# Unit 2's hidden sums in an output bank pair, all of w_out scaled by GpSimd and loaded later, and another order of the first chunk's taps, in the start of a fused convolution and feed-forward kernel

## The chip, the cores and the metric

One core of one Trainium2 chip. The metric is the device time of one execution in microseconds (us), as the median of several runs; lower is better. All runs compared here are fast (granted TensorE clock 0.999 to 1.0).

## The reference

```python
# x: (8, 4096, 192); weight: (8 heads, 7 taps); w_in: (192, 2048); w_out: (2048, 192); beta: (2048,)
w = softmax(weight, axis=-1)                    # 7 taps per head
c = causal convolution of x with w along the sequence, each head's 24 channels with its own taps
h = c.reshape(32768, 192) @ w_in
g = h / (1 + exp(-beta * h))
out = g @ w_out
```

## The kernel before

The 32768 tokens are done in 32 chunks of 1024 (512 tokens of each of two halves of the batch). For a chunk the kernel makes `ct`, the convolution, as three groups of channels. Then come 16 units: a unit is six matmuls of `ct` with 128 columns of `w_in` (*hidden*), one Silu on ScalarE over 128 x 1024 values, and *pairs* of output matmuls with `w_out`. `Silu(beta*h)` is beta times what is wanted, so `w_out` is divided by beta once, at the start (*scaling*, in four pieces).

From chunk 2 on VectorE alone makes the convolution, 7 *taps* per chunk, and a transposing DMA delivers its input. Chunks 0 and 1 are made otherwise: x is transposed on TensorE, and taps are matmuls with a diagonal matrix (chunk 0: groups 1 and 2 and part of group 3; chunk 1: group 1, called *conv1* below).

PSUM is handed out as four pairs of banks: two `ph` for the hidden sums, and `pa` and `pb` for output sums. At the start `pa` and `pb` also serve as places for transposes and taps. In the traces each engine's instructions start in the order of the Python code (in the changed kernel TensorE starts conv1's taps at 17.11 us and unit 5, which stands behind them in the code, at 18.36), so that order is what the change moves.

The parts that the change touches (cut, marked by `...`):

```python
    # loads, in this order
    ...
    for i in range(NW - 1):
        load_w_out(i)
    load(2)                      # x of the third chunk
    load_w_out(NW - 1)
    load(3)
    ...
    new_ct(0)
    for c in range(NG - 1):                                # groups 1 and 2: 7 taps on TensorE each
        pv = in_b() if c else psum_h.tile([128, 2, TOK], FP32, name="ph")
        for k in range(K):
            diag_tap(k, xt0[:, c], pv[:, 0, :])
        ...
        nc.scalar.copy(cts[0][:, c, :], pv[:, 0, :])
    ...
    K_V = 5                                                # group 3: 5 taps on VectorE, 2 on TensorE
    pv = in_a()[:, 0, :]
    for k in range(K_V, K):
        diag_tap(k, xt0[:, NG - 1], pv, k0=K_V)
    ...
    nc.vector.tensor_tensor(dst, pv, dst, ALU.add)
    ...
    scale_w_out(0)                                         # GpSimd
    scale_w_out(1)                                         # GpSimd
    ...
    CONV1 = {4: (1, 3), 5: (3, 5), 6: (5, K)}              # conv1's taps, after which unit
    ...
    first_work = {                                         # chunk 0, VectorE's work, after which unit
        4: [None, None],                                   # None: a tap of chunk 1
        5: [None],
        6: [conv1_evac, lambda: scale_w_out(2), None],     # scale 2 and 3: VectorE
        7: [None, lambda: rows_of(2)],                     # cast and transpose the third chunk
        8: [lambda: scale_w_out(3), None],
        9: [None],
    }
    QUOTA_A = {4: 2, 7: 4, 8: 4}                           # output pairs in units 4, 7, 8
    ...
            if s == 0 and u == min(CONV1):
                conv1(0, 1)                                # conv1's first tap, in front of unit 4
```

Of the kernel before, what the change touches and what calls it, by code (L numbers as in the profile page):

```python
# [9 lines left out]
FP32 = mybir.dt.float32  # L10
# [7 lines left out]
def kernel(  # L18
# [62 lines left out]
    def in_a():  # L81
        return psum_a.tile([128, 2, TOK], FP32, name="pa")

    def in_b():
        return psum_b.tile([128, 2, TOK], FP32, name="pb")
# [5 lines left out]
    def load(ch):  # L91
        p, c = divmod(ch, CHUNKS)
        xf = xf_pool.tile([128, 2, NB, D], FP32, name="xf")
        for h in range(2):
            nc.sync.dma_start(
                out=xf[:, h],
                in_=x_v[p, c * TOK : (c + 1) * TOK, h, :].rearrange(
                    "(b q) d -> q b d", q=BLK
                ),
            )  # L100
        xfs[ch] = xf
# [9 lines left out]
    def new_xt(ch):  # L111
        xt = xt_pool.tile([128, NG, HALO + TOK], BF16, name="xt")
        xts[ch] = xt
        return xt
# [31 lines left out]
    def load_w_out(i):  # L146
        fcs = slice(i * NQ, (i + 1) * NQ)
        nc.sync.dma_start(out=w_out_raw[:, fcs, :], in_=w_out_v[:, fcs, :])
# [19 lines left out]
    for r in range(2):  # L168
        nc.sync.dma_start(out=w_in_raw[r * DG : (r + 1) * DG], in_=w_in_v[:, :, 0:F0])
    load_x(x1, TOK, 1)  # L170
    for i in range(NW - 1):
        load_w_out(i)
    load(2)
    load_w_out(NW - 1)
    load(3)

    zeros = setup.tile([128, 128], BF16)
    nc.vector.memset(zeros, 0.0)
# [46 lines left out]
    def cast_rows(copy, xb, x, b):  # L225
        copy(  # L226
            xb[:, b].rearrange("q c h p -> q h c p"),
            x[:, b // 2, :, b % 2].rearrange("q h (p c) -> q h c p", c=NG),
        )
# [46 lines left out]
    for i in range(1, NW):  # L276
        load_w_in(i * FW, (i + 1) * FW)

    xt1 = setup.tile([128, HALO + TOK], FP32R)
    cts = {}  # L280

    def new_ct(s):
        cts[s] = ct_pool.tile([128, NG, TOK], BF16, name="ct")

    def diag_tap(k, xt, pv, rows=slice(0, 128), k0=0):
        o = HALO - PAD + k
        nc.tensor.matmul(  # L287
            pv,
            diag[rows, k, :],
            xt[rows, o : o + TOK],  # L290
            start=(k == k0),
            stop=(k == K - 1),
        )
# [17 lines left out]

    def scale_w_out(i):
        fcs = slice(i * NQ, (i + 1) * NQ)
        (nc.vector if i > 1 else nc.gpsimd).tensor_tensor(  # L314
            w_out_s[:, fcs, :],
            w_out_raw[:, fcs, :],
            beta_r[:, fcs].unsqueeze(2).to_broadcast((128, NQ, D)),
            ALU.mult,
        )


    new_ct(0)
    for c in range(NG - 1):
        pv = in_b() if c else psum_h.tile([128, 2, TOK], FP32, name="ph")
        for k in range(K):
            diag_tap(k, xt0[:, c], pv[:, 0, :])
        if c == 0:
            for b in range(2):
                cast_rows(nc.scalar.copy, x1b, x1, b)
        nc.scalar.copy(cts[0][:, c, :], pv[:, 0, :])  # L330
        if c == 0:
            nc.scalar.copy(w_in_s[:, :, 0:F0], w_in_raw)
    cast_rows(nc.scalar.copy, x1b, x1, 2)

    def tap(dst, src, k):
        scalar = cw[:, k : k + 1]
        if k == 0:
            nc.vector.tensor_scalar_mul(dst, src, scalar)  # L338
        else:
            nc.vector.scalar_tensor_tensor(  # L340
                out=dst, in0=src, scalar=scalar, in1=dst, op0=ALU.mult, op1=ALU.add
            )

    K_V = 5
    pv = in_a()[:, 0, :]
    for k in range(K_V, K):
        diag_tap(k, xt0[:, NG - 1], pv, k0=K_V)
    dst = cts[0][:, NG - 1, :]
    for k in range(K_V):
        o = HALO - PAD + k  # L350
        tap(dst, xt0[:, NG - 1, o : o + TOK].bitcast(FP32), k)
    nc.vector.tensor_tensor(dst, pv, dst, ALU.add)
    cast_rows(nc.vector.tensor_copy, x1b, x1, 3)
    nc.vector.reciprocal(beta_r, beta)  # L354
    scale_w_out(0)
    scale_w_out(1)


    def second():
        xt = new_xt(1)  # L360
        for i in range(2):
            pt = (in_b, in_a)[i]()
            for b in range(2):
                for c in range(NG):
                    for r in range(2):
                        rows = slice(r * DG, (r + 1) * DG)
                        o = (c * 2 + b) * DG
                        nc.tensor.matmul(
                            pt[:, r, o : o + DG],
                            x1b[rows, 2 * i + b, c].rearrange("q h p -> q (h p)"),  # L370
                            ident_b[rows, rows],
                            start=True,
                            stop=True,
                        )
            t = HALO + i * 2 * BLK
            for r in range(2):
                nc.vector.tensor_copy(
                    xt[:, :, t + r * BLK : t + (r + 1) * BLK].rearrange(
                        "p c (q b) -> p c q b", b=2
                    ),  # L380
                    pt[:, r, 0 : NG * BLK].rearrange("p (c b q) -> p c q b", c=NG, b=2),
                )
        halo(1, xt0)
        nc.vector.tensor_copy(xt1[:, HALO - PAD :], xt[:, 0, HALO - PAD :])


    CONV1 = {4: (1, 3), 5: (3, 5), 6: (5, K)}
    conv1_ps = []

    def conv1(k0, k1):  # L390
        if not conv1_ps:
            new_ct(1)
            conv1_ps.append(in_b())
        pv = conv1_ps[0]
        for k in range(k0, k1):
            for r in range(2):
                diag_tap(k, xt1, pv[:, r, :], slice(r * DG, (r + 1) * DG))
# [15 lines left out]

    gs = {}

    def hidden(s, fc, js=range(NG), ph=None):
        if fc == 0 and s not in gs:
            gs[s] = g_pool.tile([128, NF, 2, TOK], BF16, name="g")
        if ph is None:
            ph = psum_h.tile([128, 2, TOK], FP32, name="ph")  # L420
        for j in js:
            for h in range(2):
                rows = slice(h * DG, (h + 1) * DG)
                nc.tensor.matmul(  # L424
                    ph[:, h, :],
                    w_in_s[rows, j, fc * 128 : (fc + 1) * 128],
                    cts[s][rows, j, :],
                    start=(j == 0),
                    stop=(j == NG - 1),
                )  # L430
            if j == NG - 1:
                nc.scalar.activation(  # L432
                    gs[s][:, fc], ph, AF.Silu, scale=beta[:, fc : fc + 1]
                )
        return ph
# [86 lines left out]
    def rows_of(ch):  # L522
        for h in range(2):
            cast(ch, h)
        xpose(ch)
# [1 line left out]

    first_work = {
        4: [None, None],
        5: [None],  # L530
        6: [conv1_evac, lambda: scale_w_out(2), None],
        7: [None, lambda: rows_of(2)],
        8: [lambda: scale_w_out(3), None],
        9: [None],
    }

    QUOTA_A = {4: 2, 7: 4, 8: 4}
    queue = deque()
    for s in range(N_ST):
        jobs_of(s)  # L540
        for u in range(NF):
            if s == 0 and u == min(CONV1):
                conv1(0, 1)
            if s > 0 or u > 1:
                hidden(s, u)
            elif u == 0:
                phs = [hidden(0, fc, [0]) for fc in range(2)]
                for j in range(1, NG):
                    for fc in range(2):
                        hidden(0, fc, [j], phs[fc])  # L550
                second()
            if s > 0:
                output(s, u, 8 if s < N_ST - 1 else 6, "ab")
            elif u > 8:
                output(s, u, 5 if u < NF - 1 else 10, "ab")
            elif u in QUOTA_A:
                output(s, u, QUOTA_A[u], "a")
            if s == 0:
                if u in CONV1:
                    conv1(*CONV1[u])  # L560
                if u == min(CONV1):
                    queue.extend(conv_ops(1, 1))
                for work in first_work.get(u, []):
                    (work or queue.popleft())()
            else:
                if u % 2 and queue:
                    queue.popleft()()

                if u == 0 and s + 3 < N_CH:
                    load(s + 3)  # L570
                if u < 2 and s + 2 < N_CH:
                    cast(s + 2, u)
                if u == 1 and s + 2 < N_CH:
                    xpose(s + 2)
            if u == 12 and s + 2 < N_CH:
                queue.extend(conv_ops(s + 2, 0))
# [32 lines left out]
```

## Time and profile before

| | before |
|---|---|
| median time | 690.51 us (3 runs, 690.11 to 690.86); 690.43 (4 runs) with one more later |
| span of the profiled run | 688.0 us |
| TensorE busy | 99% |
| first tap on TensorE | 7.21 us |
| first Silu of chunk 0 / 1 / 2 | 12.65 / 30.25 / 51.23 us |
| every later chunk | 20.92 us per chunk |

The page's top and the head of the chain that ended last:

```profile
span 688.0 us, 24344 instructions
...
PE 682.2 (99%) x11312; PEld 521.1 (76%) x11312; DVE 524.7 (76%) x467; ACT 579.0 (84%) x530; POOL 9.9 (1%) x20
...
PE 98%; DMA 1%; ACT 0%; DVE 0%; issue 0%; ACTq 0%
```

TensorE (PE) ends last at nearly every step. A unit in the steady state is 0.65 us of hidden matmuls and 0.66 us of output matmuls. The change can only win what TensorE loses before it reaches that state, in the first 30 us. TensorE there, from the timeline (start, duration, engine, line, operation, tiles, count; in brackets the idle time before it and what ended it):

```profile
13.82 0.82 PE L424 MATMUL ph<-ct,w_in_s 64*128 64x512 bf16 x6 [0.70 <-ACT g L432]
14.82 0.82 PE L424 MATMUL ph<-ct,w_in_s 64*128 64x512 bf16 x6 [0.18 <-ACT g L432]
...
15.62 0.49 PE L287 MATMUL pb<-xt,diag 64*128 64x512 f32 x2
```

Units 2 and 3 wait 0.70 and 0.18 us for Silu to free a `ph` pair. The last line is conv1's first tap, which stands in front of unit 4. ScalarE (ACT) in the same stretch:

```profile
12.65 5.28 ACT L432 ACTIVATE g<-ph,beta 128x1024 bf16<-128x1024 f32 x5 [0.70 <-PE ph L424]
18.14 11.76 ACT L432 ACTIVATE g<-ph,beta 128x1024 bf16<-128x1024 f32 x11 [0.20 <-PE ph L424]
30.25 1.11 ACT L432 ACTIVATE g<-ph,beta 128x1024 bf16<-128x1024 f32 x1 [0.36 <-PE ph L424]
```

The first five Silus run without idle time. VectorE (DVE), GpSimd (POOL) and the DMA issues of the third chunk's transposes (SPq):

```profile
11.42 0.69 DVE L352 TENSOR_TENSOR ct<-pa,ct 128x512 bf16<-128x512 f32 x1
15.05 0.43 DVE L384 CAST xt<-xt 128x518 fp32r<-128x518 bf16 x1
15.39 1.69 DVE L338 TENSOR_SCALAR ct<-xt,cw 128x1024 bf16<-128x1024 bf16 x1
24.54 1.27 DVE L106 CAST xb<-xf 128x768 bf16<-128x768 f32 x2
32.93 1.00 DVE L338 TENSOR_SCALAR ct<-xt,cw 128x1536 bf16<-128x1536 bf16 x1
```

```profile
15.14 1.66 POOL L314 TENSOR_TENSOR w_out_s<-w_out_raw,beta_r 128x768 bf16<-128x768 f32 x1 [0.99 <-DMA w_out_raw<-in_moe_w_out_dram]
```

```profile
25.84 5.48 SPq L127 DMA_TRANSPOSE xt<-xb x4
```

The third group's sum ends at 12.11 us (11.42 + 0.69); Silu 0 follows at 12.65. The tap at 15.39 took 1.69 us with GpSimd's scaling beside it.

### The profile page before, as it was taken

To read this page: it belongs to the slowest core of one execution; us is meant where nothing else is said; L and a number is where in the kernel's file an instruction comes from. 1 tells how busy PE (TensorE), PEld (TensorE's weight loads), DVE (VectorE), ACT (ScalarE), POOL (GpSimd) and SP (SyncE) were. 2 spreads that over 40 slices of the span, in tenths; PEclk is the share of its full clock that TensorE was granted. 3 is DMA by queue.
4 is the path that set the end of the run, shared out by engine and by line. 5 is a ranking of instruction groups with operands and counts; after the bars stand their busy time and mean duration, and the time that the engine had idled before them with its cause. 6 is when DMAs were issued, how large, how long until landed. Compare 5 with 4: busy or idle time off the path is not lost.

```text
span 688.0 us, 24344 instructions
## 1 busy us (share of the span) xinstructions
PE 682.2 (99%) x11312; PEld 521.1 (76%) x11312; DVE 524.7 (76%) x467; ACT 579.0 (84%) x530; POOL 9.9 (1%) x20
## 2 busy tenths in 40 slices
PE   8999999999999999999999999999999999999998
PEld 4777777777777777777777777777777777777777
DVE  7989877788777787777797777887777977777712
ACT  7988888888888888888888888888888888888893
POOL 5000000000000000000000000000000000000000
PEclk9999999999999999999999999999999999999999
DMA  9734333244332244332444332444323443322111
GB/s 234 190 97 117 105 100 98 58 107 117 101 99 77 77 116 116 95 99 61 98 117 105 93 97 57 116 117 96 103 60 93 117 109 96 100 59 59 49 36 59
DMA packets 121861, 67.06 MB, mean 97 GB/s; under 512 B 53264, under 2 KB 121760, under 8 KB 121760
## 3 DMA queue, kind: packets, MB, share of 16 engines
q1 hardware_dynamic: 120048, 64.12, 34.7%
q0 software_dynamic: 1664, 1.38, 1.2%
q8 instruction: 88, 1.44, 0.9%
q14 instruction: 13, 0.11, 0.0%
q10 hardware_dynamic: 48, 0.01, 0.0%
HBM read 29.89 MB, written 25.17 MB: 80 GB/s over the span
## 4 chain that ended last, share of the span: by engine, by line
PE 98%; DMA 1%; ACT 0%; DVE 0%; issue 0%; ACTq 0%
PE ph L424 48%; PE pa L457 25%; PE pb L457 24%; DMA x<-in_x_dram 1%; PE pb L287 1%; ACT g L432 0%; PE ph L287 0%; DVE x0b L226 0%; ACT xt L302 0%; PE pa L287 0%; PE pb L233 0%; PE ph L233 0%; DVE diag L260 0%; ACT osb L473 0%; ACT beta L309 0%
## 5 line engine op out<-in xcount | busy, mean ns | idle before, releaser
L432 ACT ACTIVATE g<-ph,beta 128x1024 bf16<-128x1024 f32 x512 | 569.7, 1115 | 94.5 <-PE ph L424 89.8
L457 PEld LDWEIGHTS <-g 64*128 64x128 bf16 x8160 | 370.7, 94 | 102.3 <-issue 0.2
L424 PE MATMUL ph<-ct,w_in_s 64*128 64x512 bf16 x3072 | 424.3, 376 | 0.9 <-ACT g L432 0.9
L340 DVE SCALAR_TENSOR_TENSOR ct<-xt,cw,ct 128x1536 bf16<-128x1536 bf16 (+2 forms) x190 | 336.9, 1773 | 2.5
L457 PE MATMUL pa<-w_out_s,g 64*128 64x192 bf16 x4112 | 244.8, 243 | 0.0
L457 PE MATMUL pb<-w_out_s,g 64*128 64x192 bf16 (+1 forms) x4048 | 230.4, 243 | 0.0
L424 PEld LDWEIGHTS <-w_in_s 64*128 64x128 bf16 x3072 | 159.6, 94 | 54.8 <-issue 2.7
L475 DVE TENSOR_REDUCE osb<-pa 128x384 f32<-128x768 f32 x64 | 61.3, 958 | 122.5 <-PE pa L457 121.1
L475 DVE TENSOR_REDUCE osb<-pb 128x384 f32<-128x768 f32 x63 | 60.3, 957 | 29.1 <-PE pb L457 29.1
L106 DVE CAST xb<-xf 128x768 bf16<-128x768 f32 x60 | 40.5, 677 | 0.0
L338 DVE TENSOR_SCALAR ct<-xt,cw 128x1536 bf16<-128x1536 bf16 (+2 forms) x32 | 32.4, 1011 | 0.0
L473 ACT COPY osb<-pb 128x192 f32<-128x192 f32 x1 | 0.3, 319 | 7.2 <-PE pb L457 7.2
L211 POOL DMA_DIRECT2D w_in_s<-in_moe_w_in_dram x8 | 5.2, 662 | 0.0
L223 PE MATMUL ph<-zeros 128*128 128x512 bf16 (+2 forms) x11 | 4.1, 485 | 1.1 <-DVE warm L180 1.1
L287 PE MATMUL pb<-xt,diag 64*128 64x512 f32 (+1 forms) x21 | 4.7, 443 | 0.0
L121 DVE COPY xt<-xt 128x18 bf16<-128x18 bf16 x27 | 4.4, 164 | 0.0
L287 PEld LDWEIGHTS pb<-xt,diag 64*128 64x128 f32 (+1 forms) x21 | 2.7, 187 | 0.9 <-issue 0.4
L314 POOL TENSOR_TENSOR w_out_s<-w_out_raw,beta_r 128x768 bf16<-128x768 f32 x2 | 3.1, 1564 | 4.1 <-DVE beta_r L354 3.2
L223 PEld LDWEIGHTS <-zeros 128*128 128x128 bf16 x11 | 1.2, 121 | 2.2 <-issue 1.1
L181 ACT ACT_TABLE_LOAD x1 | 1.3, 1283 | 1.8 <-PEq L593 1.8
L226 ACT CAST x1b<-x 128x384 bf16<-128x384 f32 x3 | 2.0, 714 | 0.4 <-DMA x<-in_x_dram 0.4
L287 PE MATMUL ph<-xt,diag 128*128 128x512 f32 x7 | 1.9, 409 | 0.1
(55 smaller groups left out, 26.9 us busy)
## 6 DMA issues: line engine op xcount, KB each, us to landing
out_dram<-osb SPq DMA_DIRECT2D x127, 192.0 KB, 2.2
xf<-in_x_dram SPq DMA_DIRECT2D x60, 384.0 KB, 4.3
xt<-xb SPq DMA_TRANSPOSE x120, 2.6
x<-in_x_dram SPq DMA_DIRECT2D x4, 384.0 KB, 4.9
w_out_raw<-in_moe_w_out_dram SPq DMA_DIRECT2D x4, 384.0 KB, 13.5
w_in_s<-in_moe_w_in_dram POOLq DMA_DIRECT2D x6, 192.0 KB, 10.5
w_in_raw<-in_moe_w_in_dram SPq DMA_DIRECT2D x2, 192.0 KB, 5.6
w_in_s<-in_moe_w_in_dram POOLq DMA_DIRECT2D x2, 96.0 KB, 7.4
```

The source lines that it names most:

```text
L106: nc.vector.tensor_copy(xbs[ch][:, :, :, h, :], xfs[ch][:, h].rearrange("q b (p c) -> q b c p", c=NG),)
L121: nc.vector.tensor_copy(dst, last[:, :, HALO + TOK - PAD :])
L211: nc.gpsimd.dma_start(out=w_in_s[r * DG : (r + 1) * DG, :, c0:c1], in_=w_in_v[:, :, c0:c1])
L223: nc.tensor.matmul(pf[:, 0, 0:cols], zeros, zc, start=True, stop=True)
L287: nc.tensor.matmul(pv, diag[rows, k, :], xt[rows, o : o + TOK], start=(k == k0), stop=(k == K - 1),)
L314: (nc.vector if i > 1 else nc.gpsimd).tensor_tensor(w_out_s[:, fcs, :], w_out_raw[:, fcs, :], beta_r[:, fcs].unsqueeze(2).to_broadcast((12 ...
L338: nc.vector.tensor_scalar_mul(dst, src, scalar)
L340: nc.vector.scalar_tensor_tensor(out=dst, in0=src, scalar=scalar, in1=dst, op0=ALU.mult, op1=ALU.add)
L424: nc.tensor.matmul(ph[:, h, :], w_in_s[rows, j, fc * 128 : (fc + 1) * 128], cts[s][rows, j, :], start=(j == 0), stop=(j == NG - 1),)
L432: nc.scalar.activation(gs[s][:, fc], ph, AF.Silu, scale=beta[:, fc : fc + 1])
L457: nc.tensor.matmul(self.po[:, r, b * D : (b + 1) * D], g[rows, fc, self.h, q * BLK : (q + 1) * BLK], w_out_s[rows, fc, :], start=(self.don ...
L475: nc.vector.tensor_reduce(dst, self.po[:, :, 0 : nb * D].rearrange("p r n -> p n r"), axis=mybir.AxisListType.X, op=ALU.add,)
```

## The change

Its intent: start unit 0 earlier by taking one of the third group's five taps from VectorE and having TensorE do that group's share before the second group; let unit 0 be finished by itself; give unit 2's hidden sums the free pair `pa`, so that TensorE does not wait for Silu; free VectorE of the last two scalings; and load w_out later, behind what is needed first.

```diff
-    for i in range(NW - 1):
-        load_w_out(i)
-    load(2)
-    load_w_out(NW - 1)
-    load(3)
+    load_w_out(0)
 ...
+    nc.gpsimd.tensor_copy(w_out_raw[:, NQ, 0:1], x1[:, 1, 0, 0, 0:1])   # holds the next loads until x1 is in
+    for i in range(1, NW - 1):
+        load_w_out(i)
+    load(2)
+    load_w_out(NW - 1)
+    load(3)
 ...
-        (nc.vector if i > 1 else nc.gpsimd).tensor_tensor(     # scale_w_out
+        nc.gpsimd.tensor_tensor(
 ...
+    K_V = 4
+    for c, k0 in (0, 0), (2, K_V), (1, 0):                     # group 3's three taps ahead of group 2
+        for k in range(k0, K):
+            diag_tap(k, xt0[:, c], pvs[c], k0=k0)
 ...
+    for i, copy in enumerate((nc.scalar.copy, nc.vector.tensor_copy)):   # group 2's sums, in halves
+        half = slice(i * TOK // 2, (i + 1) * TOK // 2)
+        copy(cts[0][:, 1, half], pvs[1][:, half])
 ...
+    for i in range(NW):
+        scale_w_out(i)
 ...                                      # second chunk's transposes: bf16, all in one pair pb
-    CONV1 = {4: (1, 3), 5: (3, 5), 6: (5, K)}
+    CONV1 = {4: (0, 5), 5: (5, K)}
 ...
-        5: [None],
-        6: [conv1_evac, lambda: scale_w_out(2), None],
-        7: [None, lambda: rows_of(2)],
-        8: [lambda: scale_w_out(3), None],
-        9: [None],
+        5: [None, conv1_evac],
+        6: [None, None],
+        7: [None, None],
+        8: [lambda: rows_of(2)],
-    QUOTA_A = {4: 2, 7: 4, 8: 4}
+    QUOTA_A = {6: 5, 7: 5, 8: 4}
 ...
-            if s == 0 and u == min(CONV1):
-                conv1(0, 1)
 ...
-                phs = [hidden(0, fc, [0]) for fc in range(2)]
-                for j in range(1, NG):
-                    for fc in range(2):
-                        hidden(0, fc, [j], phs[fc])
+                for fc in range(2):
+                    hidden(0, fc, (0, 2, 1))                   # unit 0 by itself, group 2 last
                 second()
+            elif u == 2:
+                hidden(0, u, ph=in_a())
 ...
-                output(s, u, 5 if u < NF - 1 else 10, "ab")
+                output(s, u, 5 if u < NF - 1 else 8, "ab")
```

More of the change, by code (lines that the diff above doesn't have):

```diff
@@ L319, in scale_w_out @@
         )
-    new_ct(0)
-    for c in range(NG - 1):
-        pv = in_b() if c else psum_h.tile([128, 2, TOK], FP32, name="ph")
-        for k in range(K):
-            diag_tap(k, xt0[:, c], pv[:, 0, :])
-        if c == 0:
-            for b in range(2):
-                cast_rows(nc.scalar.copy, x1b, x1, b)
-        nc.scalar.copy(cts[0][:, c, :], pv[:, 0, :])
-        if c == 0:
-            nc.scalar.copy(w_in_s[:, :, 0:F0], w_in_raw)
-    cast_rows(nc.scalar.copy, x1b, x1, 2)
     def tap(dst, src, k):
@@ L342, in tap @@
             )
-    K_V = 5
-    pv = in_a()[:, 0, :]
-    for k in range(K_V, K):
-        diag_tap(k, xt0[:, NG - 1], pv, k0=K_V)
-    dst = cts[0][:, NG - 1, :]
+    new_ct(0)
+    K_V = 4
+    pvs = [
+        psum_h.tile([128, 2, TOK], FP32, name="ph")[:, 0, :],
+        in_b()[:, 0, :],
+        in_a()[:, 0, :],
+    ]
+    for c, k0 in (0, 0), (2, K_V), (1, 0):
+        for k in range(k0, K):
+            diag_tap(k, xt0[:, c], pvs[c], k0=k0)
+    for b in range(2):
+        cast_rows(nc.scalar.copy, x1b, x1, b)
@@ L349 @@
+    nc.scalar.copy(cts[0][:, 0, :], pvs[0])
+    nc.scalar.copy(w_in_s[:, :, 0:F0], w_in_raw)
+    cast_rows(nc.scalar.copy, x1b, x1, 2)
+    dst = cts[0][:, 2, :]
     for k in range(K_V):
         o = HALO - PAD + k
-        tap(dst, xt0[:, NG - 1, o : o + TOK].bitcast(FP32), k)
-    nc.vector.tensor_tensor(dst, pv, dst, ALU.add)
+        tap(dst, xt0[:, 2, o : o + TOK].bitcast(FP32), k)
+    nc.vector.tensor_tensor(dst, pvs[2], dst, ALU.add)
+    for i, copy in enumerate((nc.scalar.copy, nc.vector.tensor_copy)):
+        half = slice(i * TOK // 2, (i + 1) * TOK // 2)
+        copy(cts[0][:, 1, half], pvs[1][:, half])
@@ L353 @@
     cast_rows(nc.vector.tensor_copy, x1b, x1, 3)
     nc.vector.reciprocal(beta_r, beta)
-    scale_w_out(0)
-    scale_w_out(1)
+    for i in range(NW):
+        scale_w_out(i)
     def second():
         xt = new_xt(1)
-        for i in range(2):
-            pt = (in_b, in_a)[i]()
-            for b in range(2):
-                for c in range(NG):
-                    for r in range(2):
-                        rows = slice(r * DG, (r + 1) * DG)
-                        o = (c * 2 + b) * DG
-                        nc.tensor.matmul(
-                            pt[:, r, o : o + DG],
-                            x1b[rows, 2 * i + b, c].rearrange("q h p -> q (h p)"),
-                            ident_b[rows, rows],
-                            start=True,
-                            stop=True,
-                        )
+        pt = in_b().bitcast(BF16)
+        for b in range(NB):
+            for c in range(NG):
+                for r in range(2):
+                    rows = slice(r * DG, (r + 1) * DG)
+                    o = ((b // 2 * NG + c) * 2 + b % 2) * DG
+                    nc.tensor.transpose(
+                        pt[:, r, o : o + DG],
+                        x1b[rows, b, c].rearrange("q h p -> q (h p)"),
+                        ident_b[rows, rows],
+                    )
+        for i in range(2):
@@ L375, in second @@
             t = HALO + i * 2 * BLK
+            o = i * NG * BLK
             for r in range(2):
@@ L380, in second @@
                     ),
-                    pt[:, r, 0 : NG * BLK].rearrange("p (c b q) -> p c q b", c=NG, b=2),
+                    pt[:, r, o : o + NG * BLK].rearrange(
+                        "p (c b q) -> p c q b", c=NG, b=2
+                    ),
                 )
@@ L414, with hidden @@
     gs = {}
-    def hidden(s, fc, js=range(NG), ph=None):
+    def hidden(s, fc, order=range(NG), ph=None):
         if fc == 0 and s not in gs:
@@ L420, in hidden @@
             ph = psum_h.tile([128, 2, TOK], FP32, name="ph")
-        for j in js:
+        for j in order:
             for h in range(2):
@@ L427, in hidden @@
                     cts[s][rows, j, :],
-                    start=(j == 0),
-                    stop=(j == NG - 1),
+                    start=(j == order[0]),
+                    stop=(j == order[-1]),
                 )
-            if j == NG - 1:
+            if j == order[-1]:
                 nc.scalar.activation(
@@ L541 @@
         for u in range(NF):
-            if s == 0 and u == min(CONV1):
-                conv1(0, 1)
-            if s > 0 or u > 1:
+            if s > 0 or u > 2:
                 hidden(s, u)
             elif u == 0:
-                phs = [hidden(0, fc, [0]) for fc in range(2)]
-                for j in range(1, NG):
-                    for fc in range(2):
-                        hidden(0, fc, [j], phs[fc])
+                for fc in range(2):
+                    hidden(0, fc, (0, 2, 1))
                 second()
+            elif u == 2:
+                hidden(0, u, ph=in_a())
             if s > 0:
```

## The prediction

> **What bounds the kernel.** TensorE. The page has PE 99% busy of 688.0 us; the chain of waits is 98% PE. In steady state the chain shows 0.65 us of hidden matmuls plus 0.66 us of output matmuls per unit, 1.31 us; Silu takes 1.06 us back to back. 512 x 1.31 = 670 us are untouched. The change can only move what precedes chunk 1's first hidden matmul, at 29.57 us (chain). There Silu sets the pace: 16 run from 12.65 to 29.9 us with one 0.2 us gap.
>
> **Room.** From 11.12 us (first hidden matmul) PE has about 16.45 us of work (16 x 0.65 hidden, 0.45 transposes, 7 double taps x 0.213, 50 output pairs x 0.082): 2.0 us are stalls. By the timeline: about 0.65 waiting for the third group's VectorE sum (ends 12.11), 0.70 and 0.18 for Silu before units 2 and 3, the rest pacing by Silu.
>
> **Costs.**
> - One more tap on TensorE (+0.23 us), one VectorE tap less (-0.78 us). Its third-group sum should end near 11.25.
> - But the second group's sums now finish last (about 11.4), and its two half copies, on ScalarE then VectorE, read one bank. The instruction order has VectorE's wait for ScalarE's: 0.43 + 0.40 us in series. (Trainium skill, PSUM — Partial Sum Buffer, "PSUM bank collisions raise a hardware error": the compiler orders two engines on one bank.) So unit 0's last group starts about 12.35 and Silu 0 about 12.85: 0.2 later.
> - Unit 2's sums in the other pair: it no longer waits for Silu 0. -0.70.
> - Second chunk's evacuation starts about 13.65 instead of 12.98; conv1's taps wait for its cast, about 16.1: a PE stall near 0.5 us.
> - w_out scaling leaves VectorE (-2 x 0.95 us) for GpSimd (1.5-1.7 us each). Chunk 1's ct is ready by 28 instead of 29.26, so the last quota can be 8 instead of 10 pairs; 52 instead of 50 pairs are done by then (+0.16 us credit).
> - w_out pieces 1-3 are issued at about 9.8 us, behind GpSimd's w_in issues (end 9.5); piece 1 should land about 15-16.5 (before 15.1).
>
> **Sum.** Chunk 1 starts about 29.05 (-0.5) with two more pairs done: gain about 0.65 us.
>
> **Main risk.** The Trainium skill (SBUF — State Buffer, "Who interferes with whom") says that VectorE's fast copies and two-input ops and a GpSimd op that reads SBUF fully block each other. The trace agrees: a 1024-element scaling of VectorE took 1.69 us beside GpSimd's 1.66 us scaling, while 1536 elements take 1.01 alone. If w_out piece 1 lands just before the cast that conv1 needs (about 15.7), that cast, conv1 and PE lose up to 1.3 us and the gain is gone. If later, taps block, and conv1's evacuation ends about 21.9, just before unit 9's outputs need that pair (22.2).
>
> **Prediction.** 690.0 us, range 689.2 to 690.9; faster by over 2% 0.01, within 2% 0.98, slower 0.01.
>
> **Right if the profile shows:** Silu 0 at 12.6-13.1; no 0.7 us idle before unit 2; one PE wait before conv1's first tap; VectorE's half copy after ScalarE's; chunk 1's first hidden matmul at 28.8-29.3; four GpSimd scalings, some slowing VectorE ops; then 1.31 us per unit as before.
>
> **Wrong if:** the half copies overlap (Silu 0 near 12.4; gain about 1.1); GpSimd blocks conv1's cast (conv1 at 17 or later, no gain or a loss); w_out piece 3 lands after 26 us; or the steady state shifts phase.

## More of the kernel before

The cast at 15.05 is conv1's input; it ends at 15.48, and conv1's first tap starts 0.15 us later (15.62; 147 ns unrounded). The third chunk's casts run at 24.54, its transposes are issued from 25.84, and when VectorE reaches that chunk's first tap at 32.93 it does not wait (no bracket).

## The result, and the profile after

| | before | after |
|---|---|---|
| median time, same rounds | 690.43 us (4 runs, 690.11 to 690.86) | 690.79 us (4 runs, 690.04 to 691.01) |
| ratio, 95% interval | | 1.0003 (0.9986 to 1.002) |
| five more rounds, in a later group | 690.15 (9 runs) | 690.31 (5 runs), ratio 1.0001 (0.9988 to 1.0013) |

The ratios are of fast runs of the same rounds; they are not quite the ratios of the medians quoted. By time the two kernels are the same; the range of the prediction held, but its gain of 0.65 us did not come. Runs of one kernel scatter by up to 1.6 us within a group (in the last group one run of before by 3.8), so timing can't settle a few tenths; the traces can, stage by stage.

For that the span is cut at four points that every trace has: the first tap on TensorE (T), the first Silu of chunks 1, 2 and 31, and the end. Each kernel was profiled twice (all values in us, differences of starts read from the traces):

| stage | before | before again | after | after again |
|---|---|---|---|---|
| start to T | 7.21 | 7.52 | 7.91 | 7.04 |
| T to chunk 1's first Silu | 23.04 | 22.98 | 23.23 | 23.44 |
| chunk 1's to chunk 2's | 20.98 | 20.98 | 21.30 | 21.38 |
| chunk 2's to chunk 31's | 606.68 | 606.67 | 606.68 | 606.67 |
| to the end | 30.07 | 30.07 | 29.95 | 29.96 |
| T to the end | 680.77 | 680.70 | 681.16 | 681.45 |

The start varies by up to 0.9 us with the changed kernel alone (7.91 and 7.04). From T on, by the means of the two profiles, the change costs 0.33 us in chunk 0 and 0.36 us in chunk 1, and gets 0.11 back at the end for the two output pairs it did early: 0.57 us in all, 0.08% of the time.

The head of the page and of its chain after:

```profile
span 689.1 us, 24349 instructions
...
PE 93%; DVE 4%; DMA 1%; SPq 1%; ACT 0%; issue 0%; DVEq 0%
```

The chain that ended last is no longer nearly all TensorE's: VectorE has 4% of it, and the issue and landing of DMAs (SPq, DMA) 2%. TensorE after (this profile's T is 7.91, so subtract 0.70 to compare with before):

```profile
13.04 1.04 PE L430 MATMUL ph<-ct,w_in_s 64*128 64x512 bf16 x8 [0.38 <-DVE ct L357]
...
14.25 0.83 PE L430 MATMUL pa<-ct,w_in_s 64*128 64x512 bf16 x6
14.90 1.63 PE L430 MATMUL ph<-ct,w_in_s 64*128 64x512 bf16 x12
17.11 1.44 PE L291 MATMUL pb<-xt,diag 64*128 64x512 f32 x10 [0.58 <-DVE xt L390]
```

The waits of 0.70 and 0.18 us for Silu are gone, as meant. In their place TensorE waits for VectorE's half copy (line 357) before unit 0's last group, and 0.58 us for conv1's input (line 390). ScalarE after:

```profile
12.16 0.37 ACT L357 CAST ct<-pb 128x256 bf16<-128x256 f32 x1
13.53 2.12 ACT L438 ACTIVATE g<-ph,beta 128x1024 bf16<-128x1024 f32 x2 [1.00 <-PE ph L430]
15.54 1.11 ACT L438 ACTIVATE g<-pa,beta 128x1024 bf16<-128x1024 f32 x1
16.54 2.13 ACT L438 ACTIVATE g<-ph,beta 128x1024 bf16<-128x1024 f32 x2
19.25 11.70 ACT L438 ACTIVATE g<-ph,beta 128x1024 bf16<-128x1024 f32 x11 [0.59 <-PE ph L430]
31.14 1.11 ACT L438 ACTIVATE g<-ph,beta 128x1024 bf16<-128x1024 f32 x1 [0.19 <-PE ph L430]
```

The first five Silus again run without idle time and at the same pace (Silus of units 0 to 3 at 13.53, 14.54, 15.54, 16.54; before 12.65, 13.66, 14.68, 15.69). Then ScalarE stands 0.59 us before Silu 5, because the wait for conv1 stands in front of unit 5 in TensorE's order. VectorE after:

```profile
11.46 0.69 DVE L354 TENSOR_TENSOR ct<-pa,ct 128x512 bf16<-128x512 f32 x1
12.56 0.42 DVE L357 CAST ct<-pb 128x256 bf16<-128x256 f32 x1 [0.41 <-ACT ct L357]
16.54 0.43 DVE L390 CAST xt<-xt 128x518 fp32r<-128x518 bf16 x1
16.88 0.48 DVE L328 TENSOR_SCALAR ct<-xt,cw 128x1024 bf16<-128x1024 bf16 x1
28.68 1.26 DVE L106 CAST xb<-xf 128x768 bf16<-128x768 f32 x2
37.31 1.01 DVE L328 TENSOR_SCALAR ct<-xt,cw 128x1536 bf16<-128x1536 bf16 x1 [3.43 <-DMA xt<-xb]
```

The half copy waits 0.41 us for ScalarE's, as the prediction had read from the instruction order. conv1's input (16.54) is ready at 16.97; its first tap starts at 17.11, again 147 ns later. The third chunk's casts come at 28.68 instead of 24.54, and the first tap of that chunk then waits 3.43 us for its transposes. The chain shows what that does (start, duration, what):

```profile
21.34 1.30 DVE ct L330
22.66 2.38 DVE ct L330
25.06 1.30 DVE ct L330
26.38 2.37 DVE ct L330
28.75 1.19 DVE xb L106 x2
30.03 1.24 SPq L127
...
33.91 3.27 DMA xt<-xb
...
49.64 1.83 DVE ct L330
51.52 0.82 PE ph L430 x6
```

From 21.34 to 51.5 us each link releases the next: four taps of chunk 1, the casts, the transposes, seven taps of chunk 2, and only then chunk 2's first hidden matmul. Followed further back, the chain is VectorE from 14.47 us on, and before that the second chunk's transposes on TensorE, the hidden matmuls of units 0 and 1 and the two half copies. Before, the same stretch of the chain is TensorE alone. Two of the four taps take 2.4 instead of 1.3 us; GpSimd's scalings run beside them:

```profile
21.94 2.00 POOL L318 TENSOR_TENSOR w_out_s<-w_out_raw,beta_r 128x768 bf16<-128x768 f32 x1 [0.61 <-DMA w_out_raw<-in_moe_w_out_dram]
25.88 1.79 POOL L318 TENSOR_TENSOR w_out_s<-w_out_raw,beta_r 128x768 bf16<-128x768 f32 x1 [1.94 <-DMA w_out_raw<-in_moe_w_out_dram]
```

### The profile page after: what moved, and what is told of

Read it like the earlier page. It is cut to its first block, busy times and chain, and to the rows that moved or that the text cites. A ratio compares the mean times of both kernels' runs of the same rounds, so it can differ in the third digit from the quotient of the medians.

```text
span 689.1 us, 24349 instructions
## 1 busy us (share of the span) xinstructions
PE 682.9 (99%) x11313; PEld 499.9 (73%) x11313; DVE 523.0 (76%) x465; ACT 578.0 (84%) x530; POOL 13.9 (2%) x23
## 4 chain that ended last, share of the span: by engine, by line
PE 93%; DVE 4%; DMA 1%; SPq 1%; ACT 0%; issue 0%; DVEq 0%
PE ph L430 45%; PE pa L463 24%; PE pb L463 23%; DVE ct L330 3%; SPq L127 1%; DMA xt<-xb 0%; PE ph L219 0%; DVE xt L381 0%; DMA w<-in_weight_dram 0%; PE ph L291 0%; DVE xb L106 0%; DVE osb L481 0%; PE pb L291 0%; DVE ct L328 0%; DVE ct L409 0%; ACT xt L306 0%
## 5 line engine op out<-in xcount | busy, mean ns | idle before, releaser
L463 PEld LDWEIGHTS <-g 64*128 64x128 bf16 x8160 | 355.9, 94 | 117.1 <-issue 0.2
L430 PE MATMUL ph<-ct,w_in_s 64*128 64x512 bf16 x3066 | 416.0, 376 | 0.5 <-DVE ct L357 0.4
L463 PE MATMUL pa<-w_out_s,g 64*128 64x192 bf16 x4112 | 239.2, 243 | 0.0
L463 PE MATMUL pb<-w_out_s,g 64*128 64x192 bf16 (+1 forms) x4048 | 225.4, 243 | 0.0
L430 PEld LDWEIGHTS <-w_in_s 64*128 64x128 bf16 x3072 | 145.0, 94 | 61.5 <-issue 1.4
L318 POOL TENSOR_TENSOR w_out_s<-w_out_raw,beta_r 128x768 bf16<-128x768 f32 x4 | 6.8, 1704 | 9.3 <-DMA w_out_raw<-in_moe_w_out_dram 7.3
L381 DVE COPY xt<-pb 128x384 bf16<-128x384 bf16 x4 | 2.0, 550 | 1.0 <-PE pb L372 1.0
```

The lines of the kernel that those rows point to most:

```text
L318: nc.gpsimd.tensor_tensor(w_out_s[:, fcs, :], w_out_raw[:, fcs, :], beta_r[:, fcs].unsqueeze(2).to_broadcast((128, NQ, D)), ALU.mult,)
L430: nc.tensor.matmul(ph[:, h, :], w_in_s[rows, j, fc * 128 : (fc + 1) * 128], cts[s][rows, j, :], start=(j == order[0]), stop=(j == order[-1]),)
L463: nc.tensor.matmul(self.po[:, r, b * D : (b + 1) * D], g[rows, fc, self.h, q * BLK : (q + 1) * BLK], w_out_s[rows, fc, :], start=(self.don ...
```

## The experiments

Twelve runs were made, in four groups; those of a group shared a chip and its runs of the kernel before. Times of stages come from the one profile of each run. "T" is the first tap, as above.

### 1. b_again: the kernel before, a second profile

No edit.

> The kernel before, unchanged, profiled a second time. Theory 1 (the start jitters): the two profiles before and after already differ by 0.70 us at the first tap on TensorE (7.21 and 7.91 us), ahead of anything that the change touches, because the small weight DMA landed later; then this second profile of the same kernel may start its first tap anywhere from 7.2 to 8.0 us, and from the first tap on it repeats the first profile to 0.1 us (Silu of chunk 1's unit 0 comes 23.04 us after the first tap, chunk 2's 20.98 us after that). Rival (the change itself delays the start): the first tap is at 7.2 again, within 0.1.

Measured: T at 7.52 us, then 22.98 and 20.98. The rival falls: the start moves by itself (by 0.31 us here) and the rest repeats to 0.1 us. Over all 14 profiles T lies between 7.04 and 7.91 us, both ends of it in profiles of the changed kernel. In the first profile after, the weights' small DMA released TensorE's first real matmul at 2.87 us instead of 2.45; in the other profiles that is not the cause, and what moves them was not followed further. So the 0.70 us between the first two profiles' starts is not shown to be an effect of the change.

### 2. a_again: the changed kernel, a second profile and five rounds

No edit.

> The changed kernel, unchanged, again, with five rounds. Theory 1 (the start jitters, and behind it the change costs 0.4 us: +0.19 in chunk 0, +0.32 in chunk 1, -0.12 for two pairs fewer at the end): first tap anywhere from 7.2 to 8.0 us, chunk 1's first Silu 23.23 us after it, chunk 2's 21.3 us after that, and the ratio of times near 1.0005. Rival (the change delays the start): first tap at 7.9 again and a ratio near 1.0015.

Measured: T at 7.04, then 23.44 and 21.38; ratio 1.0001 (0.9988 to 1.0013). The rival falls. Chunk 0 cost 0.2 us more than in the first profile, most of it for piece 1 of w_out: its scaling started at T + 12.25 (11.86 in the first profile), and unit 7's ten output matmuls, standing for it, take 0.78 us instead of 0.61; Silu 15 comes 16.47 us after Silu 0 instead of 16.30.

### 3. a_rows: the third chunk's casts and transposes earlier

```diff
-        7: [None, None],
-        8: [lambda: rows_of(2)],
+        7: [lambda: rows_of(2), None],
+        8: [None],
```

> The changed kernel with the casts and transposes of the third chunk issued in unit 7, ahead of the last two taps of chunk 1, instead of behind all of them in unit 8. Theory (the third chunk's transposes leave 4 us late, at 30.0 instead of 25.8 us, so the first tap of chunk 2 waits 3.4 us for their DMA and chunk 2's first hidden matmul comes 0.32 us late): VectorE no longer waits for the transposes (below 0.5 us), chunk 2's first Silu comes 20.9 to 21.0 us after chunk 1's instead of 21.3, and chunk 1's stays at 23.2 us after the first tap. Rival (the 0.32 us come from the sums leaving the output pairs, or from the later w_out): 21.3 us again.

Measured: 23.20 and 20.98; T to end 680.84; 690.09 us (5 runs), ratio 0.9999 (0.9985 to 1.0012). VectorE's lines of the casts and of the chunk's first tap:

```profile
24.57 1.26 DVE L106 CAST xb<-xf 128x768 bf16<-128x768 f32 x2
33.38 1.01 DVE L328 TENSOR_SCALAR ct<-xt,cw 128x1536 bf16<-128x1536 bf16 x1
```

The tap no longer waits. The loss in chunk 1 is fully explained by the later transposes: one line of order gives it back.

### 4. b_u2: unit 2's pair, with unit 0 by itself and the transposes in one pair, in the kernel before

```diff
-                phs = [hidden(0, fc, [0]) for fc in range(2)]
 ...
+                for fc in range(2):
+                    hidden(0, fc)
                 second()               # as in the change: all transposes in one pair, pb; unit 0 in the old order of groups
+            elif u == 2:
+                hidden(0, u, ph=in_a())
```

> The kernel before with one part of the change alone: the second chunk's transposes in one pair, unit 0 by itself, and unit 2's sums in the other output pair; the taps, the w_out loads and scaling, the order of the work and the quotas stay as before. Theory A (Silu sets the pace from its first instruction on, so TensorE's 0.70 and 0.18 us of waiting for Silu were slack): the 0.70 us before unit 2 vanish from the profile, but Silu 15 starts no earlier than 16.1 us after Silu 0 as before, and chunk 1's first Silu comes 23.0 us or more after the first tap. Theory B, the prediction's (each removed wait of TensorE is time won): chunk 1's first Silu comes about 22.3 us after the first tap.

Measured: no wait before units 2 and 3. Silu 0 to Silu 3 take 3.01 us where they took 3.04 before. T to chunk 1's first Silu 23.43 (before 23.04); 690.85 us (4 runs), ratio 1.001 (0.9996 to 1.0023). TensorE:

```profile
13.75 0.83 PE L425 MATMUL pa<-ct,w_in_s 64*128 64x512 bf16 x6
14.40 0.83 PE L425 MATMUL ph<-ct,w_in_s 64*128 64x512 bf16 x6
16.61 0.50 PE L287 MATMUL pb<-xt,diag 64*128 64x512 f32 x2 [1.39 <-DVE xt L385]
```

Theory B falls. Without 0.88 us of TensorE's waits, Silus 0 to 3 take 0.03 us less: ScalarE had work all that time. TensorE runs ahead and meets the next thing it needs, conv1's input, and waits there instead, 1.39 us. Finishing unit 0 by itself did bring Silu 0 forward (T + 5.21; before 5.44 and 5.36), but conv1's first tap came at T + 8.79 (before 8.41), because VectorE's copies of the second chunk now start behind all 24 transposes, in one pair, instead of behind the first 12 (T + 6.15; before 5.77). That these parts cost 0.4 us has its reason there: the kernel before has conv1's first tap in front of unit 4, so ScalarE ran dry too, 0.65 us before Silu 4.

### 5. a_act: the second group's sums copied whole

```diff
-    for i, copy in enumerate((nc.scalar.copy, nc.vector.tensor_copy)):
-        half = slice(i * TOK // 2, (i + 1) * TOK // 2)
-        copy(cts[0][:, 1, half], pvs[1][:, half])
+    nc.scalar.copy(cts[0][:, 1, :], pvs[1])
```

> The changed kernel with the second group's sums copied whole by ScalarE instead of in halves by ScalarE and then VectorE. Theory (the two halves read one bank, so they run one after the other: 0.37 + 0.42 us, and two operations' fixed cost is all that the split buys): the wait of TensorE for unit 0's last group ends 0.2 us earlier, Silu 0 comes 5.35 to 5.5 us after the first tap instead of 5.62 and 5.67, chunk 1's first Silu about 23.0 instead of 23.2 to 23.4. Rival (the split works as meant, the copies overlap in part): Silu 0 comes at 5.6 or later.

Measured: Silu 0 at T + 5.34 (5.62 and 5.67 in the changed kernel), chunk 1's first Silu at T + 22.94. The whole copy:

```profile
12.08 0.59 ACT L355 CAST ct<-pb 128x512 bf16<-128x512 f32 x1 [0.39 <-PE pb L291]
```

One whole copy takes 0.59 us; the halves, 0.37 and 0.42 with a wait between, take 0.82 from the first's start to the second's end (12.16 to 12.98). The split costs, as the theory has it. But chunk 2 came 21.61 us later, at T + 44.55, where it was (44.53 and 44.82), and T to the end took 681.20: what was won in chunk 0 was lost again. VectorE reached the third chunk's casts 0.29 us sooner (T + 20.48 instead of 20.77), but its first tap of that chunk began at T + 29.42 (29.40), because the transposes landed no earlier. In the five profiles in which TensorE waits for VectorE at chunk 2 (the changed kernel's two, a_act, a_early_w, a_pa5), its first Silu follows that tap by 15.13 or 15.14 us.

### 6. a_wdve: w_out pieces 2 and 3 scaled by VectorE again

```diff
-        nc.gpsimd.tensor_tensor(
+        (nc.vector if i > 1 else nc.gpsimd).tensor_tensor(
 ...
-        7: [None, None],
-        8: [lambda: rows_of(2)],
+        7: [lambda: scale_w_out(2), None, None],
+        8: [lambda: scale_w_out(3), lambda: rows_of(2)],
```

> The changed kernel with w_out pieces 2 and 3 scaled by VectorE again, between the taps of chunk 1 in units 7 and 8; pieces 0 and 1 stay on GpSimd. Theory (GpSimd's scaling holds up VectorE's two-input taps for about as long as VectorE would need for the scaling itself, so the move freed nothing): each tap of chunk 1 takes 1.28 to 1.31 us, none 2.3 us as two of four did in the changed kernel, the two scalings cost 0.96 us each, and from the evacuation of conv1 to the third chunk's first cast there are 7.1 to 7.4 us where the changed kernel has 7.4. Chunk 2's first Silu comes 21.1 to 21.4 us after chunk 1's as in the changed kernel. Rival (the move took 1.9 us off VectorE): that stretch becomes 9.3 us, and chunk 2 comes 1.5 us or more later than in the changed kernel.

VectorE's four taps and two scalings:

```profile
20.93 2.60 DVE L330 SCALAR_TENSOR_TENSOR ct<-xt,cw,ct 128x1024 bf16<-128x1024 bf16 x2
23.46 0.95 DVE L318 TENSOR_TENSOR w_out_s<-w_out_raw,beta_r 128x768 bf16<-128x768 f32 x1
24.32 2.60 DVE L330 SCALAR_TENSOR_TENSOR ct<-xt,cw,ct 128x1024 bf16<-128x1024 bf16 x2
```

Measured: every tap takes 1.3 us. From the first of the four taps to the third chunk's first cast there are 6.78 us (20.93 to 27.71), although VectorE does both scalings in them; in the changed kernel 7.34 (21.34 to 28.68). That is below the range expected, in the theory's direction: with GpSimd scaling, VectorE lost 2.15 us to longer taps (2.38 + 2.37 less 2 x 1.30) to be spared 1.9 us of work. Chunk 1 came late, at T + 23.76, because TensorE's output pairs of unit 10 had to wait for piece 2; so chunk 2 followed after 20.98 us, not the 21.1 to 21.4 expected, at T + 44.74, within the changed kernel's 44.53 to 44.82. T to the end took 681.38: the sooner casts won nothing here.

### 7. a_early_w: all w_out loads early again

```diff
-    load_w_out(0)
+    for i in range(NW - 1):
+        load_w_out(i)
+    load(2)
+    load_w_out(NW - 1)
+    load(3)
 ...
-    nc.gpsimd.tensor_copy(w_out_raw[:, NQ, 0:1], x1[:, 1, 0, 0, 0:1])     # and the loads after it
```

> The changed kernel with all w_out loads issued at the start as before, so that piece 1 lands near 8.0 us after the first tap instead of 10.3 to 12.3. Theory (the Vector engine's fast cast and GpSimd's scaling exclude each other, as my prediction feared; the later loads are what keeps them apart): GpSimd's second scaling starts 8.0 us after the first tap, conv1's cast (at 8.6 in the changed kernel) stretches from 0.43 to more than 1 us or starts only after it, conv1's first tap comes 9.8 us or more after the first tap instead of 9.2, and chunk 1's first Silu at 23.7 or later. Rival (the loads were deferred for the sake of DMA bandwidth, and GpSimd does not matter here): conv1's first tap stays at 9.2 and chunk 1's first Silu at 23.2 to 23.4.

Measured: conv1's first tap at T + 9.19 as in the changed kernel (9.20), chunk 1's first Silu at T + 23.31. My theory falls: GpSimd's second scaling started at T + 9.3, not 8.0, just behind conv1's cast, which kept its 0.43 us. The overlap that the prediction's main risk names came just too late to touch conv1's cast: VectorE's next two-input tap, beside that scaling, took 2.37 us. What a scaling beside the cast itself would cost is not tested. From T to the end this run took 681.68 us, longer than the changed kernel; chunk 2's first tap waited 3.84 us for its transposes. The early loads also brought a wait that the changed kernel does not have:

```profile
16.25 0.82 PE L428 MATMUL ph<-ct,w_in_s 64*128 64x512 bf16 x5 [0.59 <-DMA w_in_s<-in_moe_w_in_dram]
```

The wait for w_in is hidden here behind the wait for conv1. It suggests what the deferral is for: w_in comes late when w_out is loaded beside it. (The Trainium skill, DMA: Bandwidth & Descriptors, "Issuing engines are not separate DMA queues", says that the DMAs of all issuing engines run on the same 16 and interleave; w_in is issued by GpSimd and w_out by SyncE, and this wait agrees.)

### 8 and 9. a_pa5 and a_pa5_rows: unit 5 into the wait for conv1

```diff
-    CONV1 = {4: (0, 5), 5: (5, K)}
+    CONV1 = {5: (0, 5), 6: (5, K)}
-            if s > 0 or u > 2:
+            if s > 0 or u > 2 and u != 5:
-            elif u == 2:
+            elif u in (2, 5):                  # unit 5's sums in pa, ahead of conv1
                 hidden(0, u, ph=in_a())
 # first_work one unit later; a_pa5_rows also has rows_of(2) in unit 7
```

> The changed kernel with unit 5's sums put in the free output pair too, ahead of the taps of conv1, which move behind it into units 5 and 6. Theory 1 (in the changed kernel TensorE stands 0.58 us before conv1's taps and ScalarE then 0.6 us before Silu 5, because conv1's input comes late and stands in front of unit 5 in TensorE's order): the wait of ScalarE before Silu 5 vanishes, Silu 15 comes 15.3 to 15.7 us after Silu 0 instead of 16.3 to 16.5, and chunk 1's first Silu 22.5 to 22.8 us after the first tap instead of 23.2 to 23.4. Theory 2 (chunk 2 waits for VectorE's chain, not for chunk 1): chunk 2's first Silu stays at 44.5 to 44.8 us after the first tap as in the changed kernel (44.53 and 44.82), so the whole gain is lost again and the time stays within 0.3 us. Rival to 2: chunk 2 follows 21.3 us after chunk 1, and 0.6 us are won.

> The same with the third chunk's casts and transposes in unit 7 as in the earlier run. If both theories hold, chunk 1's first Silu comes 22.5 to 22.9 us after the first tap and chunk 2's 20.9 to 21.0 after that, and from the first tap to the end there are 680.2 us or less (before: 680.70 and 680.77; changed: 681.16 and 681.45). The ratio to before would be about 0.9992, so within its interval of 1. If chunk 1's data from VectorE are then too late (two casts ahead of its last two taps), chunk 1's Silu comes at 23.1 or later instead.

Measured for a_pa5: the idle time before Silu 5 is gone (Silus 0 to 6 run 1.00 us apart), but chunk 1's first Silu came at T + 24.41, later. New waits follow: 0.38 us for Silu 5 to free `pa` for output sums, and

```profile
22.19 0.34 PE L463 MATMUL pa<-w_out_s,g 64*128 64x192 bf16 x4 [0.93 <-POOL w_out_s L318]
```

for piece 1 of w_out, whose scaling started only at 20.68 us in this run, when the piece had landed. T to the end took 682.65. Theory 1 held for the gap and failed for the sum; theory 2 can't be judged, since chunk 1 was not early.

For a_pa5_rows: chunk 2 followed 20.98 us after chunk 1, but chunk 1 came at T + 25.18; 690.61 us (5 runs, 690.35 to 691.73), ratio 1.0007 (0.9993 to 1.002). The profiled run was the slowest of the five: the second half of x1 landed only at 12.3 us, ScalarE waited 0.98 us for it with group 2's half copy behind it, and TensorE 1.80 us (T to the end 682.81). So that profile does not answer its question. It shows another weakness of the change: it put ScalarE's cast of x1 ahead of the copy that unit 0 needs.

### 10. best1: three repairs

```diff
-    cast_rows(nc.scalar.copy, x1b, x1, 2)
-    for i, copy in enumerate((nc.scalar.copy, nc.vector.tensor_copy)):
-        half = slice(i * TOK // 2, (i + 1) * TOK // 2)
-        copy(cts[0][:, 1, half], pvs[1][:, half])
-    cast_rows(nc.vector.tensor_copy, x1b, x1, 3)
+    nc.scalar.copy(cts[0][:, 1, :], pvs[1])
+    for b in range(2, NB):
+        cast_rows(nc.vector.tensor_copy, x1b, x1, b)
 ...
-        7: [None, None],
-        8: [lambda: rows_of(2)],
+        7: [lambda: rows_of(2), None],
+        8: [None],
```

> The changed kernel with three repairs: the second group's sums copied whole by ScalarE, the third block of x1 cast by VectorE after its sum (so that ScalarE's copy no longer stands behind the landing of x1), and the third chunk's transposes issued in unit 7. If the repairs add up: Silu 0 5.3 to 5.45 us after the first tap, chunk 1's first Silu 22.9 to 23.0, chunk 2's 20.98 after that, and 680.4 to 680.7 us from the first tap to the end (before 680.70 and 680.77, changed 681.16 and 681.45). The time then equals that of before within 0.3 us: three repairs undo the loss but win nothing.

Measured: Silu 0 at T + 5.37, chunk 1 at T + 22.97, chunk 2 20.99 later, T to end 680.59; 690.45 us (5 runs, 689.93 to 690.66) beside 690.67 of before, ratio 0.9998 (0.9985 to 1.001). All as expected: the repairs undo the loss and win 0.1 to 0.2 us from T on in this one profile, which the times can't confirm.

### 11 and 12. best2 and best3: unit 5 once more, with w_out earlier or with fewer pairs

```diff
 # both: the repairs of best1 and unit 5 in pa as in a_pa5_rows
 # best2: w_out piece 1 loaded early; QUOTA_A = {7: 5, 8: 5}
 # best3: pieces 1 to 3 late as in the change; QUOTA_A = {7: 4, 8: 4}
```

> The same repairs, and unit 5's sums in the free pair with conv1's taps behind it, w_out piece 1 loaded early again (in the earlier run with unit 5 in that pair TensorE stood 0.93 us for its late scaling), and no output pairs before unit 7. If TensorE's wait before conv1 was the last idle time that can be filled: no gap of ScalarE from Silu 0 to Silu 8 above 0.2 us, chunk 1's first Silu 22.3 to 22.7 us after the first tap, and 680.0 to 680.4 us from the first tap to the end; a ratio of 0.999 to before. If work only moves about (5 pairs fewer done in chunk 0 have to be done later), 680.6 or more.

Measured for best2: T to end 681.60, 690.60 us (5 runs), ratio 1.0002 (0.9988 to 1.0015). With piece 1 early, w_in is late, and this time nothing hides it:

```profile
16.65 0.82 PE L429 MATMUL ph<-ct,w_in_s 64*128 64x512 bf16 x5 [1.09 <-DMA w_in_s<-in_moe_w_in_dram]
```

> The kernel with the three repairs (680.59 us from first tap to end), and again unit 5's sums in the free pair ahead of conv1's taps, but with w_out pieces 1 to 3 loaded late as in the changed kernel, and only 4 output pairs in each of units 7 and 8, so that none needs piece 1 before unit 9. Theory (TensorE's wait before conv1 is idle time that unit 5 can fill, if neither w_in nor w_out piece 1 is then missing): no gap of ScalarE above 0.2 us between Silu 0 and Silu 15, chunk 1's first Silu 22.3 to 22.7 us after the first tap, 680.0 to 680.4 us from first tap to end, a ratio near 0.999. Rival (the loads at the start are the limit: w_in, w_out and x1 share them, and whatever is moved forward waits for one of them): a new wait for a DMA or for GpSimd's scaling appears and 680.6 us or more remain.

Measured for best3: Silus 0 to 9 run without a gap above 0.2 us, 9.15 us in all where the changed kernel takes 9.98 (13.53 to 23.51) and the kernel before 9.77. So the wait for conv1 was what held these Silus up. Then TensorE stands for the scaling of w_out:

```profile
23.16 0.59 PE L461 MATMUL pa<-w_out_s,g 64*128 64x192 bf16 x10 [1.43 <-POOL w_out_s L318]
...
25.57 0.34 PE L461 MATMUL pa<-w_out_s,g 64*128 64x192 bf16 x4 [0.92 <-POOL w_out_s L318]
```

T to end 682.95; 691.09 us (6 runs, 690.80 to 691.99), ratio 1.0006 (0.999 to 1.0022). The profiled run is again the slowest of its runs, and the scaling of piece 1 started only at 21.30 us in it, when the piece had landed. The second wait is for the scaling of piece 2, which GpSimd began at 23.07, behind piece 1's, and which took 2.44 us beside VectorE's taps. The rival holds: what was moved forward ended at a new wait, for w_in in one order and for w_out's landing and scaling in the other. No version beats the kernel before by more than the runs scatter.

## Why the prediction was right or wrong

The time lay in the stated range (690.79 in 689.2 to 690.9), and "within 2%" was right. But the predicted gain of 0.65 us was a loss of 0.57 us from the first tap on. A range as wide as the scatter of the runs hid that: that the time fell inside it is luck as far as the account goes, since the sum had the wrong sign.

**The bound: right from chunk 2 on.** TensorE bounds both kernels there, and both take 606.7 us to chunk 31's first Silu. In the start of the changed kernel the chain is VectorE's.

**Silu 0 later by 0.2 us: right.** Predicted 12.85 with T at 7.21, so T + 5.64; measured T + 5.62 and 5.67 against 5.44 and 5.36. The mechanism was right too: the half copies run in series. The Trainium skill (PSUM — Partial Sum Buffer, "PSUM bank collisions raise a hardware error") says that the compiler puts two engines' accesses to one bank in order, and the trace agrees: VectorE's half starts at 12.56, after ScalarE's ended at 12.53. a_act shows that the split costs. That the one bank is the reason was not tested by halves in two banks; writing one tile is not the reason, since ScalarE's copy of group 1 into `ct` (9.84 to 10.42) ran beside VectorE's taps into it (from 9.03). The third group's sum did end 0.66 us earlier counted from T, but it stopped being the last thing unit 0 needs: a gain turned into a new wait.

**"Unit 2's sums in the other pair: it no longer waits for Silu 0. -0.70.": the step that failed.** The wait was real and is gone, but it was slack, for two reasons. First, ScalarE was busy throughout it, and the Silus of units 0 to 3 start 1.0 us apart with or without it (b_u2: 3.01 us for the three steps instead of 3.04). Second, TensorE next needs conv1's input. In both profiles of the kernel before conv1's first tap starts 147 ns after the cast of its input ends, and so it does in the changed kernel, where TensorE visibly stands for it; so that tap came about as early as its input allowed, and time won ahead of it had nowhere to go. In b_u2 it turned into a wait of 1.39 us. The first reason is shown by b_u2; the second is read from the equal lags. The prediction had said itself that Silu sets the pace there, and then still booked TensorE's wait for Silu as time won.

**conv1's wait near 0.5 us: right in size (0.58), and not charged.** The predicted -0.5 us for chunk 1 is just the 0.2 of Silu 0 less the 0.70. But the change brought conv1's first tap from T + 8.41 to T + 9.20, and the wait for it starves ScalarE for 0.59 us before Silu 5; best3, where unit 5 fills it, runs Silus 0 to 9 in 9.15 us instead of 9.98. By the means of two profiles, Silu 0 came 0.24 us later, Silu 15 another 0.25 later, and chunk 1's first Silu 0.16 sooner after Silu 15, where unit 15 has 8 pairs instead of 10: 0.33 us later in all, not 0.5 us earlier.

**"Then 1.31 us per unit as before": right for the units, wrong where chunk 2 begins.** The Silus of chunk 1 are 1.31 us apart in both kernels; only the last step, to chunk 2's first Silu, takes 1.68 and 1.76 us instead of 1.37. The order of the third chunk's transposes was in the diff and was not costed: they left 3.4 us later counted from T (29.97 less 7.91 instead of 25.84 less 7.21), and chunk 2 came 0.36 us late. a_rows gives all of it back. Without that repair a gain in chunk 0 vanishes there, as a_act showed.

**Scaling on GpSimd: the price was named and not charged.** The prediction counted 1.9 us off VectorE. The Trainium skill (SBUF — State Buffer, "Who interferes with whom") says that a VectorE op with two SBUF inputs and a GpSimd op that reads SBUF block each other fully. The trace agrees: 2.38 and 2.37 us for taps of 1.30. a_wdve shows the balance: VectorE needs 0.56 us less up to the casts when it does the scaling itself.

**w_out piece 1 at 15 to 16.5 us: mis-sized.** The scaling that waits for it started at 19.77 (19.07 on the clock of before). GpSimd's small copy had to wait for x1 and ran at 11.36 (10.66 on the clock of before), not 9.8. In a_again that lateness cost about 0.17 us (experiment 2). The feared block of conv1's cast did not happen; a_early_w shows that it would not have with early loads either, though by a margin of only about 0.2 us (the scaling at T + 9.3, the cast from T + 8.6 to 9.1).

**The credit of two pairs: right**, 0.11 us measured, 0.16 predicted.

What stays open: what moves the first tap between 7.04 and 7.91 us; why the transposes, issued later, also took longer to land (the chain has 3.27 us for the last of them, 3.58 in a_act; the median of all transposes on the page of before is 2.6); and whether unit 5 ahead of conv1 pays when both w_in and w_out are there in time, which no run had.

## What to carry to other kernels

A wait of the bounding engine is worth something only if the engine it waits for is idle meanwhile and what it needs next is already there; look at that engine's line, and at the next input, before booking the wait as a gain. When a change reorders one engine's queue to speed up the next stage, follow the queue to the stage after it: here the work that was moved behind other work was what chunk 2 needed. And where run times scatter more than the effect, cut the traces at common events and compare stage by stage; two profiles of each kernel told more than nine timed runs.

## What the Trainium skill lacked or had wrong

- SBUF — State Buffer ("Who interferes with whom"): its rule holds, also for the three-operand taps. It has no figure for this pair: a bf16 tap of 128x1024 grew from 1.30 to 2.38 us, and GpSimd's 128x768 scaling, 1.47 us alone, took up to 2.00 us beside VectorE's taps in the changed kernel, so both sides paid.
- PSUM — Partial Sum Buffer ("PSUM bank collisions raise a hardware error"): right; it doesn't draw the consequence that splitting the copy of one bank between two engines costs time. Halves in series took 0.82 us, a whole copy by ScalarE 0.59 us.
- No page has the scatter of a kernel's start: the first tap of nearly the same start code came between 7.04 and 7.91 us in 14 profiles, while the stretch from there to the end of one kernel repeated to 0.07 us (before) and 0.29 us (after).
- DMA: Bandwidth & Descriptors ("Issuing engines are not separate DMA queues"): agrees with the runs; what it means for a start in which every load is urgent it leaves open. Here with w_out piece 1 moved forward TensorE waited 1.09 us for w_in (best2), and with it moved back 1.43 us for the scaling of that piece (best3).
